# Value products in blocks of eight and four units, nine probability buffers, and another order at the end and in the norm, in an adaLN block with windowed attention

## The chip, the cores and the metric

The kernel runs on one core of one Trainium2 chip. The metric is device time in microseconds (us), measured from outside the program. The times shown are medians of a few runs. A profiled execution also gives its span, from the first to the last instruction on the core, which is a little shorter than the time of the same execution measured from outside.

## What is computed

The input is one sequence of S = 2048 rows with D = 448 features. The reference, cut to what matters:

```python
mod = (silu(c) @ w_mod).reshape(1, 6, 1, D)       # sa, ca, ga, sb, cb, gb
h = layernorm(x) * (1 + ca) + sa
qkv = h @ wqkv                                     # 16 heads of 28
scores = q @ k.T * 28 ** -0.5                      # key j is seen by query i if 0 <= i - j < 256
x = x + ga * (softmax(scores) @ v @ wo)
h = layernorm(x) * (1 + cb) + sb
x = x + gb * (mish(h @ w1 + b1) @ w2)              # w1: 448 x 1792
```

## The kernel before, in words

Each matrix product of width D is done in three passes: both operands are split into a high and a low part, and high x high, high x low and low x high are summed (`passes`, L205). The sequence is cut into four groups of 512 rows (`NG`, `GT`). The program is one list of instructions, written out by hand: a Python function issues an instruction when it is called, and each engine takes its own in the order in which they were issued (L76, a manual schedule). So the order of the calls is the schedule.

**Attention.** A group has 16 heads, and a group with a head is an item `i` (`NS` = 64 items). For each item the program does the following. `L` (L671) loads the item's queries and keys from a scratch tensor in DRAM. `A` (L680) makes the scores of 128 queries against 384 keys on the tensor engine (PE) into one of three banks `sA`, and the vector engine (DVE) takes the row maximum with the mask added (L689); there are four such quarters per item. After two items, `M1` (L697) splits the eight columns of maxima on DVE (L700, L701). `M2` (L703) transposes them on PE (tile `mt`, L705), copies the result on DVE (`mr`, L707), and sends it by DMA into two more rows of the query tile, so that a product of keys and queries comes out with the maximum already subtracted. `B` (L720) makes these transposed scores. An item has three units, and unit `u` covers one block set `b` of 512 columns (L22). `B` first puts the mask into the bank `sB`, either by PE with an identity matrix (L759) or, where `seeds(u)` is true, by a copy that the scalar engine (ACT) made two units earlier (L739). Then it multiplies (L731), and ACT takes the exponential into a tile `P` (L734).

Twelve units, three block sets of four heads, make a round `q`. There are 16 rounds, four to a group, and `r` is the unit's place in its round. `PV` (L761) multiplies the probabilities with the values: four heads fill the four column quarters of the array, each with 32 columns, into one bank `pv`. In the kernel before it is called once for each block set, that is for four units, at the places `PV_AT` (L1123): units 7, 9 and 13 counted from the start of the round. After the third, `EV` (L773) copies the sum out on ACT, `E` (L777) transposes it (tile `et`), and `E2` (L783) divides by the row sums on DVE.

**What stands between the units.** The loop at L1124 goes through the units. At each it calls `place` at up to six slots: the table `scores` (L1109) tells at which unit of the round and at which slot the 16 quarters `A` of the next round go, `M2_AT` (L1110) the same for `M2`, and `OUT_AT` (L1112) for `E` and `E2`. Between them a filler is drawn (`fill_main`, L994): the next group's projections to queries, keys and values (tiles `qk`, `qk_v`), and the last group's output projection (`ot`, `wo`). `RATE` (L1049) is how much filler a unit gets, one number for each group. `load_slot` (L1070) issues the loads of queries and keys on the DMA queue of SP, in which the DMA of `M2` stands too.

**Feed-forward.** The loop at L1227 goes through `NN` = 56 steps, 14 column blocks of 128 in each of the four groups. A step does `f1_mm` (11 products into a bank `z`, L970), `f1_act` (ACT: Mish into `t`, L976, and its high part `ah`, L977; DVE: the low part `al`, L978), and `ff2` of the step before (three products for each of four row tiles into four banks `acc`, L1191 to L1193). In the last step of a group, `ff2` also multiplies each bank with the gate (`yo`, L1197), adds the residual (L1200) and stores it. In the last group, three of these adds are on GpSimd (POOL), and the fourth is shared by DVE and POOL. The tiles `yo` come from three buffers with the tag `xr` (L548). A second filler (L1220) runs along in `fill_step` (L1222): what is left of the attention's output, and the second layer norm of the next group, whose transposes are 64 instructions on DVE, issued by fours (`blocks`, L892, the transposes at L897). In the first group a step draws it four times.

## Time and profile before

| | |
|---|---|
| time, median of 3 runs | 663.73 us (661.86, 663.73, 669.27) |
| the profiled execution | 668.01 us, span 666.2 us |
| PE, matmuls | 634.8 us busy, 3712 |
| DVE | 391.1 us busy, 1138 |
| ACT | 335.6 us busy, 584 |
| POOL | 120.6 us busy, 173 |
| mean granted clock of PE | 0.983 of full speed |

Rows of the timeline give the start, the duration, the engine, the line, the operation with the tiles it writes and reads, and how many instructions were merged into the row; in brackets stands how long the engine was idle before, and what ended that. Products of fp32 tiles appear as two hardware instructions each, so a block of eight `pv` products has 16 of them. A window's row gives the busy time of PE, of its weight loads (PEld), DVE, ACT and POOL, the granted clock of PE, and the DMA share and rate. Attention lasts from about 38 us to 366 us, and the feed-forward from there to the end.

### The profile page before, as it was taken

The page shows a single profiled execution, that of the slowest core. Times are in us where ns is not written, and L with a number is a line of the kernel's source. Part 1 is how long each engine was busy: PE and PEld are TensorE (multiplying, and loading weights), DVE is VectorE, ACT ScalarE, POOL GpSimd, SP SyncE. Part 2 cuts the span into 40 slices and gives each one's busy share as a digit, 9 for nine tenths or more (in the row PEclk, how much of TensorE's full clock was granted, in tenths as well). Part 3 has the DMA queues.
Part 4 walks back from the last instruction along what each step waited for, and adds up shares of the span by engine and source line. Part 5 has one row for each costly group of instructions (what it writes and reads, how often), then busy time and mean ns, then how long its engine had stood idle before and what let it go on. Part 6 is the DMA issues. An engine that isn't in the chain of part 4 may idle for free.

```text
span 666.2 us, 10727 instructions
## 1 busy us (share of the span) xinstructions
PE 634.8 (95%) x3712; PEld 514.3 (77%) x3712; DVE 391.1 (59%) x1138; ACT 335.6 (50%) x584; POOL 120.6 (18%) x173
## 2 busy tenths in 40 slices
PE   3998999999999999999988999999999999999996
PEld 3786777677887678877756898878888888888885
DVE  5765686675678767578777334954584438631112
ACT  4544567588875778635668633432233224323221
POOL 6652000043011200000030445340021001100002
PEclk9997999599999999999999999999999999999999
DMA  8786676547754478435852853003000300010001
GB/s 215 211 233 215 225 245 213 147 114 227 270 172 142 141 224 307 147 110 151 235 150 69 261 148 106 11 1 111 0 1 0 112 1 0 1 55 1 1 0 55
DMA packets 49169, 83.77 MB, mean 126 GB/s; under 512 B 5838, under 2 KB 27612, under 8 KB 49116
## 3 DMA queue, kind: packets, MB, share of 16 engines
q1 hardware_dynamic: 49116, 83.10, 40.6%
q8 instruction: 29, 0.48, 0.3%
q14 instruction: 24, 0.20, 0.1%
HBM read 53.45 MB, written 29.36 MB: 124 GB/s over the span
## 4 chain that ended last, share of the span: by engine, by line
PE 74%; issue 11%; DVE 8%; DMA 3%; ACT 2%; SPq 1%; POOL 1%; POOLq 0%; DVEq 0%; ACTq 0%
PE z L970 15%; PE qk L321 10%; PE pv L769 7%; PE sA L687 6%; PE sB L731 6%; PE wo L321 5%; PE acc L1193 4%; PE acc L1191 4%; PE acc L1192 4%; PE qk_v L321 4%; DVE yt L897 3%; DMA k<-scr 2%; PE sB L759 2%; DVE junk L689 1%; PE qk L506 1%
## 5 line engine op out<-in xcount | busy, mean ns | idle before, releaser
L689 DVE CUSTOM_DVE_ANT_0 junk<-sA,strip 128x384 bf16<-128x384 f32 (+2 forms) x256 | 135.4, 529 | 80.6 <-PE sA L687 65.8
L734 ACT ACTIVATE P<-sB 128x512 f32<-128x512 f32 (+2 forms) x192 | 108.3, 570 | 84.5 <-PE sB L731 82.1
L978 DVE TENSOR_TENSOR al<-t,ah 128x512 fp32r<-128x512 f32 x56 | 41.2, 735 | 137.2 <-ACT ah L977 136.9
L976 ACT ACTIVATE t<-z,b1c 128x512 f32<-128x512 f32 x56 | 38.4, 686 | 156.8 <-PE z L970 145.0
L970 PE MATMUL z<-hhf,w 128*128 128x512 f32 x224 | 88.9, 397 | 0.0
L970 PE MATMUL z<-hlf,w 128*128 128x512 f32 x224 | 88.8, 397 | 0.0
L731 PE MATMUL sB<-q,k 86*128 86x384 f32 (+1 forms) x352 | 87.2, 323 | 0.7 <-ACT sB L739 0.7
L687 PE MATMUL sA<-k,q 84*128 84x384 f32 (+2 forms) x256 | 82.4, 360 | 4.3 <-DMA k<-scr 2.7
L1193 PE MATMUL acc<-w2h,al 128*128 128x448 f32 x224 | 82.1, 366 | 1.9 <-DVE al L978 1.9
L1191 PE MATMUL acc<-w2h,ah 128*128 128x448 f32 x224 | 81.9, 366 | 0.0
L1192 PE MATMUL acc<-w2l,ah 128*128 128x448 f32 x224 | 81.8, 365 | 0.0
L731 PEld LDWEIGHTS sB<-q,k 86*128 86x128 f32 x352 | 60.3, 197 | 11.1 <-ACT sB L739 4.4
L970 PE MATMUL z<-hhf,w1l 128*128 128x512 f32 x168 | 66.5, 396 | 0.0
L897 DVE STREAM_TRANSPOSE yt<-xn 32x128 f32<-32x128 f32 x192 | 58.1, 302 | 2.6
L687 PEld LDWEIGHTS sA<-k,q 84*128 84x128 f32 x256 | 48.4, 197 | 10.4 <-DVE mx L689 2.7
L739 ACT ACTIVATE sB<-strip 128x512 f32<-128x512 bf16 (+2 forms) x95 | 54.6, 575 | 3.0
L769 PE MATMUL pv<-P,v 128*32 128x256 f32 (+2 forms) x704 | 50.2, 399 | 0.4 <-DVE on L790 0.4
L970 PEld LDWEIGHTS z<-hlf,w 128*128 128x128 f32 x224 | 42.1, 188 | 10.1
L970 PEld LDWEIGHTS z<-hhf,w 128*128 128x128 f32 x224 | 42.1, 188 | 9.1 <-issue 0.6
L1193 PEld LDWEIGHTS acc<-w2h,al 128*128 128x128 f32 x224 | 42.1, 188 | 5.9 <-DVE al L978 2.6
L1191 PEld LDWEIGHTS acc<-w2h,ah 128*128 128x128 f32 x224 | 42.1, 188 | 5.0
L1192 PEld LDWEIGHTS acc<-w2l,ah 128*128 128x128 f32 x224 | 42.1, 188 | 4.7
(155 smaller groups left out, 1029.1 us busy)
## 6 DMA issues: line engine op xcount, KB each, us to landing
k<-scr SPq DMA_DIRECT2D x48, 252.0 KB
q<-scr SPq DMA_DIRECT2D x64, 168.0 KB
scr<-st SPq DMA_DIRECT2D x21, 512.0 KB
scr<-st SPq DMA_DIRECT2D x29, 256.0 KB
x<-x1d SPq DMA_DIRECT2D x10, 448.0 KB
xin<-in_A_x_dram SPq DMA_DIRECT2D x8, 448.0 KB
xr<-in_A_x_dram SPq DMA_DIRECT2D x16, 224.0 KB
x1d<-xr SPq DMA_DIRECT2D x16, 224.0 KB
```

Of the source, the lines that this page charges most:

```text
L321: PE.matmul(p, b, a, start=(n == 0), stop=(n == 10))
L687: PE.matmul(p[:, c0:384], q[0:84, t * 128:(t + 1) * 128], k[0:84, t * 128 + c0:t * 128 + 384], start=True, stop=True)
L689: DVE.tensor_tensor_reduce(out=junk[:, c0:384], in0=p[:, c0:384], in1=mask[:, c0:384], scale=1.0, scalar=-3.0e38, op0=ALU.add, op1=ALU.max ...
L731: PE.matmul(p[:, c:c + 128 * (t1 - t0)], k[:, jj * 128:(jj + 1) * 128], q[:, t0 * 128:t1 * 128], start=False, stop=True, skip_group_check= ...
L734: ACT.activation(P[:, c0:], p[:, c0:], AF.Exp, scale=SCALE)
L739: ACT.activation(p[:, c0:], strip[:, c + c0:c + 512], AF.Copy)
L769: PE.matmul(pvb[q][32 * a:32 * a + 32, t0 * 128:t1 * 128], V[j % NV][:, h + a, :], Pt[4 * w + a][:, c:c + 128 * (t1 - t0)], start=(b == 0 ...
L897: DVE.transpose(y4[32 * j:32 * j + 32, ci, :, 32 * i:32 * i + 32], x4[32 * i:32 * i + 32, :, ci, 32 * j:32 * j + 32])
L970: PE.matmul(zb[n], ps[m][1], ps[m][0], start=(m == 0), stop=(m == 10))
L1191: PE.matmul(p, ah[n][:, ts], w2h[f], start=(f == 0), stop=False)
L1192: PE.matmul(p, ah[n][:, ts], w2l[f], start=False, stop=False)
L1193: PE.matmul(p, al[n][:, ts], w2h[f], start=False, stop=(f == NF - 1))
```

## The change

The places of `PV`. It is now called twice in a round, at units 9 and 13: first for the block sets 0 and 1 together (eight units of four heads), then for block set 2 (four units). The tile `P` gets nine buffers for seven. The 16 quarters `A` of a round, `M2` and `E` have other places, and the loop has other numbers of the mask copies that ACT makes (99 in all for 95). `RATE` has a number for each round instead of each group.

Here is PE's order in the first round, in which a block set has one piece for each head, with the block sets 0 and then 1. `pv` is the value product, `sA` are the quarters, `mt` the transposed maxima. Before, block set 0:

```order
L321 MATMUL qk_3_766<-hh_566,wq_88 128x512
L769 MATMUL pv_774<-P_661,v_152 32x384
L769 MATMUL pv_774<-P_677,v_152 32x384
L769 MATMUL pv_774<-P_698,v_152 32x384
L769 MATMUL pv_774<-P_714,v_152 32x384
L705 MATMUL mt_779<-ident,ms_740 16x128
```

and, some rows later, block set 1:

```order
L321 MATMUL qk_3_766<-hh_566,wq_88 128x512
L687 MATMUL sA_0_811<-k_7_381,q_3_393 128x128
L769 MATMUL pv_774<-P_728,v_154 32x256
L769 MATMUL pv_774<-P_746,v_154 32x256
L769 MATMUL pv_774<-P_755,v_154 32x256
L769 MATMUL pv_774<-P_787,v_154 32x256
L759 LDWEIGHTS identr
```

In the changed kernel:

```order
L321 MATMUL qk_3_763<-hh_566,wq_88 128x512
L687 MATMUL sA_0_806<-k_7_381,q_3_393 128x128
L687 MATMUL sA_1_809<-k_7_381,q_3_393 128x256
L770 MATMUL pv_812<-P_661,v_152 32x384
L770 MATMUL pv_812<-P_680,v_152 32x384
L770 MATMUL pv_812<-P_701,v_152 32x384
L770 MATMUL pv_812<-P_714,v_152 32x384
L770 MATMUL pv_812<-P_728,v_154 32x256
L770 MATMUL pv_812<-P_746,v_154 32x256
L770 MATMUL pv_812<-P_755,v_154 32x256
L770 MATMUL pv_812<-P_777,v_154 32x256
L687 MATMUL sA_2_821<-k_7_381,q_3_393 128x384
```

The first four products have moved down to the second four, with no other product between them, and `sA_1`, of the quarters, has moved up ahead of them, while `sA_2` follows directly behind. `mt` no longer stands behind a block of `pv`.

The feed-forward's filler. In the first group a step now draws it four times up to step 4, then five times, and three times as soon as the normalised tiles of the second group exist. This is DVE's order in that part: `L897`, in the changed kernel `L898`, are the transposes of the second group's norm, with their number at the end of the row, and `al` is the low part for the next `ff2`. Before:

```order
L897 STREAM_TRANSPOSE yt_5117<-xn_1_5046 32x4x32 x16
L978 TENSOR_TENSOR al_5212<-t_5213,ah_5211 128x512
L883 TENSOR_SCALAR yt_5117<-yt_5117,cols 128x512
L897 STREAM_TRANSPOSE yt_5117<-xn_1_5046 32x4x32 x16
L978 TENSOR_TENSOR al_5265<-t_5266,ah_5264 128x512
L883 TENSOR_SCALAR yt_5117<-yt_5117,cols 128x512
L897 STREAM_TRANSPOSE yt_5117<-xn_1_5046 32x4x32 x16
L978 TENSOR_TENSOR al_5318<-t_5319,ah_5317 128x512
L883 TENSOR_SCALAR yt_5117<-yt_5117,cols 128x512
L978 TENSOR_TENSOR al_5355<-t_5356,ah_5354 128x512
L978 TENSOR_TENSOR al_5389<-t_5390,ah_5388 128x512
L978 TENSOR_TENSOR al_5423<-t_5424,ah_5422 128x512
```

In the changed kernel:

```order
L898 STREAM_TRANSPOSE yt_5114<-xn_1_5043 32x4x32 x4
L982 TENSOR_TENSOR al_5249<-t_5250,ah_5248 128x512
L898 STREAM_TRANSPOSE yt_5114<-xn_1_5043 32x4x32 x12
L982 TENSOR_TENSOR al_5296<-t_5297,ah_5295 128x512
L884 TENSOR_SCALAR yt_5114<-yt_5114,cols 128x512
L898 STREAM_TRANSPOSE yt_5114<-xn_1_5043 32x4x32 x12
L982 TENSOR_TENSOR al_5345<-t_5346,ah_5344 128x512
L898 STREAM_TRANSPOSE yt_5114<-xn_1_5043 32x4x32 x4
L884 TENSOR_SCALAR yt_5114<-yt_5114,cols 128x512
L982 TENSOR_TENSOR al_5386<-t_5387,ah_5385 128x512
L982 TENSOR_TENSOR al_5420<-t_5421,ah_5419 128x512
```

Between two `al` stood 16 transposes and stand at most 12 now, and the last transposes come one `al` later.

The end. `ff2` of the steps 53, 54 and 55 is put off until the products `z` of step 55 are issued, and is then done row tile by row tile: two tiles of step 53 first, then for each row tile what is left of the three steps. `ah` and `al` of step 55 get buffers of another tag. The adds of the last group are all on DVE. PE's last 12 rows before were these (`acc3_0` to `acc3_3` are the banks of the four row tiles; `ah55` and `al55` are the parts of the last step):

```order
L1191 MATMUL acc3_0_6542<-w2h13_5394,ah55_6900 128x448
L1192 MATMUL acc3_0_6542<-w2l13_5395,ah55_6900 128x448
L1193 MATMUL acc3_0_6542<-w2h13_5394,al55_6901 128x448
L1191 MATMUL acc3_1_6543<-w2h13_5394,ah55_6900 128x448
L1192 MATMUL acc3_1_6543<-w2l13_5395,ah55_6900 128x448
L1193 MATMUL acc3_1_6543<-w2h13_5394,al55_6901 128x448
L1191 MATMUL acc3_2_6544<-w2h13_5394,ah55_6900 128x448
L1192 MATMUL acc3_2_6544<-w2l13_5395,ah55_6900 128x448
L1193 MATMUL acc3_2_6544<-w2h13_5394,al55_6901 128x448
L1191 MATMUL acc3_3_6545<-w2h13_5394,ah55_6900 128x448
L1192 MATMUL acc3_3_6545<-w2l13_5395,ah55_6900 128x448
L1193 MATMUL acc3_3_6545<-w2h13_5394,al55_6901 128x448
```

In the changed kernel 30 rows from the end:

```order
L1195 MATMUL acc3_0_6539<-w2h12_5350,ah54_6867 128x448
L1196 MATMUL acc3_0_6539<-w2l12_5351,ah54_6867 128x448
L1197 MATMUL acc3_0_6539<-w2h12_5350,al54_6868 128x448
L1195 MATMUL acc3_0_6539<-w2h13_5391,ah55_6885 128x448
L1196 MATMUL acc3_0_6539<-w2l13_5392,ah55_6885 128x448
L1197 MATMUL acc3_0_6539<-w2h13_5391,al55_6886 128x448
L1195 MATMUL acc3_1_6540<-w2h12_5350,ah54_6867 128x448
L1196 MATMUL acc3_1_6540<-w2l12_5351,ah54_6867 128x448
L1197 MATMUL acc3_1_6540<-w2h12_5350,al54_6868 128x448
L1195 MATMUL acc3_1_6540<-w2h13_5391,ah55_6885 128x448
L1196 MATMUL acc3_1_6540<-w2l13_5392,ah55_6885 128x448
L1197 MATMUL acc3_1_6540<-w2h13_5391,al55_6886 128x448
```

Row tile 0 is complete behind the sixth of these rows and row tile 1 behind the last; 18 rows for the tiles 2 and 3 follow, nine for each.

The whole diff:

```diff
@@ -546,7 +546,7 @@
     wol = [mid.tile([128, D], F32R, name=f"wol_{i}", tag="wo", bufs=7) for i in range(3)]
 
     def xr_tile(name):
-        return mid.tile([128, 512], F32, name=name, tag="xr", bufs=3)
+        return mid.tile([128, D], F32, name=name, tag="xr", bufs=3)
 
 
     def stg(pl, name):
@@ -730,7 +730,7 @@
         for jj, t0, t1, c in by_width(bl)[::-1]:
             PE.matmul(p[:, c:c + 128 * (t1 - t0)], k[:, jj * 128:(jj + 1) * 128], q[:, t0 * 128:t1 * 128],
                       start=False, stop=True, skip_group_check=True)
-        P = Pt[u] = att.tile([128, 512], F32, name=f"P{u}", tag="P", bufs=7)
+        P = Pt[u] = att.tile([128, 512], F32, name=f"P{u}", tag="P", bufs=9)
         ACT.activation(P[:, c0:], p[:, c0:], AF.Exp, scale=SCALE)
         if seeds(u + 2):
             p = sb[u + 2] = bank(f"sB{u % 2}", 1, f"sB{u + 2}")
@@ -741,7 +741,7 @@
     sb, known = {}, {}
 
     def seeds(u):
-        if not 12 <= u < NU or not ((0, 2730, 4095, 1365, 640, 4095, 4095, 1365, 0, 4095, 4095, 1365, 0, 1365, 84, 0)[u // 12] >> (u % 12)) & 1:
+        if not 12 <= u < NU or not ((0, 2746, 4095, 1365, 642, 4093, 4095, 1365, 0, 4095, 4095, 1367, 0, 1373, 592, 2048)[u // 12] >> (u % 12)) & 1:
             return False
         i, b = unit(u)
         return units(i // H, b)[0][3] >= known[u % 2]
@@ -759,16 +759,17 @@
             PE.matmul(p[:, c:c + n], identr, strip[:, m:m + n], start=(i == 0), stop=False, skip_group_check=True)
 
     def PV(w):
-        q, b = divmod(w, 3)
+        q, e = divmod(w, 2)
         g, h = divmod(4 * q, H)
-        if b == 0:
+        if e == 0:
             pvb[q] = bank("pv", 1, f"pv{q}")
-        for n, (jj, t0, t1, c) in enumerate(by_width(units(g, b))):
-            j = 4 * g - 2 + jj
-            for a in range(4):
-                PE.matmul(pvb[q][32 * a:32 * a + 32, t0 * 128:t1 * 128], V[j % NV][:, h + a, :],
-                          Pt[4 * w + a][:, c:c + 128 * (t1 - t0)],
-                          start=(b == 0 and n == 0), stop=False, skip_group_check=True)
+        for b in ((0, 1), (2,))[e]:
+            for n, (jj, t0, t1, c) in enumerate(by_width(units(g, b))):
+                j = 4 * g - 2 + jj
+                for a in range(4):
+                    PE.matmul(pvb[q][32 * a:32 * a + 32, t0 * 128:t1 * 128], V[j % NV][:, h + a, :],
+                              Pt[12 * q + 4 * b + a][:, c:c + 128 * (t1 - t0)],
+                              start=(b == 0 and n == 0), stop=False, skip_group_check=True)
 
     def EV(q):
         O4[q] = att.tile([128, GT], F32, name=f"o4_{q}", tag="o4")
@@ -971,7 +972,10 @@
 
     def f1_act(n):
         f = n % NF
-        ah[n], al[n] = ftile("ah", n, F32R), ftile("al", n, F32R)
+        if n == NN - 1:
+            ah[n], al[n] = (FW["ff"].tile([128, GT], F32R, name=f"{x}{n}", tag="stg", bufs=6) for x in ("ah", "al"))
+        else:
+            ah[n], al[n] = ftile("ah", n, F32R), ftile("al", n, F32R)
         t = ftile("t", n)
         ACT.activation(t, zb[n], AF.Mish, bias=FW["b1c"][:, f:f + 1])
         ACT.activation(ah[n], t, AF.Copy)
@@ -1046,14 +1050,14 @@
         if not (told.get(i) == "bank" and pipe.held() or told.get(i) == "dve" and two):
             told[i] = next(side[i], None)
 
-    RATE = (0.76, 1.01, 0.88, 0.45)
+    RATE = (0.76, 0.76, 0.72, 0.76, 1.01, 1.01, 1.01, 1.09, 0.92, 0.96, 0.91, 0.88, 0.45, 0.6, 0.45, 0.41)
     FRONT = (0, 1, 3, 0)
     ln1 = {g: gen_ln1(g, g == 1) for g in range(1, NG)}
     fillers = {g: fill_main(g) for g in range(NG)}
     side = (fill_early(), fill_late())
 
-    def step(g):
-        return next(fillers[g], 99.0) or RATE[g]
+    def step(g, q):
+        return next(fillers[g], 99.0) or RATE[q]
 
     def need(keys, g):
         if all((g, m) in done for m in keys):
@@ -1106,10 +1110,10 @@
             load_slot(4 + i)
     later[:0] = late
     credit = 0.0
-    scores = {(0, 3): [0], (0, 4): [1], (2, 0): [2], (2, 5): [3], (3, 0): [4], (4, 0): [5], (4, 5): [6], (5, 0): [7], (6, 1): [8], (6, 3): [9], (7, 3): [10], (8, 3): [11], (8, 5): [12], (9, 1): [13], (9, 5): [14], (10, 1): [15]}
-    M2_AT = {(7, 0): 0, (11, 3): 1}
-
-    OUT_AT = {(3, 5): E, (4, 2): E2}
+    scores = {(0, 3): [0], (0, 5): [1], (1, 0): [2], (1, 4): [3], (3, 0): [4], (4, 0): [5], (4, 4): [6], (5, 0): [7], (6, 1): [8], (7, 0): [9], (7, 5): [10], (8, 3): [11], (8, 5): [12, 13], (9, 0): [14], (9, 1): [15]}
+    M2_AT = {(7, 1): 0, (11, 4): 1}
+
+    OUT_AT = {(4, 1): E, (4, 2): E2}
 
     def place(q, r, slot):
         if (r, slot) in OUT_AT and 0 < q <= NS // 4:
@@ -1120,7 +1124,7 @@
             A(4 * q + 4 + n // 4, n % 4)
         if (r, slot) in M2_AT:
             M2(2 * q + 2 + M2_AT[r, slot])
-    PV_AT = {4 * w + (7, 5, 5)[w % 3]: w for w in range(NU // 4)}
+    PV_AT = {12 * q + (9, 13)[e]: 2 * q + e for q in range(NS // 4) for e in range(2)}
     for u in range(NU + 7):
         s, k = divmod(u, 3)
         g = s // H
@@ -1131,8 +1135,8 @@
         w = PV_AT.get(u)
         if w is not None:
             PV(w)
-            if w % 3 == 2:
-                EV(w // 3)
+            if w % 2:
+                EV(w // 2)
         q, r = divmod(u, 12)
         place(q, r, 0)
         if u < NU:
@@ -1149,10 +1153,10 @@
                 chunk["v"] = 4 if v == 0 and g or 0 < g < NG - 1 else 2
             if v == 0:
                 credit = 0.0
-            credit += RATE[g] * (2 if v < FRONT[g] else 1)
+            credit += RATE[q] * (2 if v < FRONT[g] else 1)
             n = 0
             while credit > 0.0:
-                credit -= step(g)
+                credit -= step(g, q)
                 n += 1
                 if n == 1:
                     place(q, r, 3)
@@ -1181,11 +1185,11 @@
     FW["ff"] = ff
     p1, gbn = FW["p1"], FW["gbn"]
 
-    def ff2(n):
+    def ff2(n, tiles=range(4)):
         g, f = divmod(n, NF)
         if f == 0:
             acc[g] = [bank("acc", 4, f"acc{g}_{t}") for t in range(4)]
-        for t in range(4):
+        for t in tiles:
             ts = slice(t * 128, (t + 1) * 128)
             p = acc[g][t][:, 0:D]
             PE.matmul(p, ah[n][:, ts], w2h[f], start=(f == 0), stop=False)
@@ -1195,9 +1199,7 @@
                 j = 4 * g + t
                 y = xr_tile(f"yo{j}")[:, 0:D]
                 DVE.tensor_tensor(y, p, gbn, op=ALU.mult)
-                for eng, a, b in (((DVE, 0, D),) if g < NG - 1 else ((POOL, 0, D),) if t < 3 else
-                                  ((DVE, 0, 256), (POOL, 256, D))):
-                    eng.tensor_tensor(y[:, a:b], y[:, a:b], x1[g][:, t, a:b], op=ALU.add)
+                DVE.tensor_tensor(y, y, x1[g][:, t, :D], op=ALU.add)
                 dma(of[j * 128:(j + 1) * 128, :], y)
 
     def gen_x1_ln2(g):
@@ -1241,8 +1243,14 @@
             pieces(n)
         if n:
             fill_step()
-            ff2(n - 1)
-            for _ in range(2 + (g == 0)):
+            if n == NN:
+                ff2(n - 3, (0, 1))
+                for t in range(4):
+                    for last in range(n - 3 + (t < 2), n):
+                        ff2(last, (t,))
+            elif n < NN - 2:
+                ff2(n - 1)
+            for _ in range(2 + (g == 0 and 1 not in XN2) * (1 + (n > 4))):
                 fill_step()
     for st in (ff_s, mid_s, cst_s, FW["s"], psf_s):
         st.close()
```

## The prediction, made before the changed kernel ran

> **What bounds the kernel now.** I read the head of the page first, then the chain that ended last.
>
> ```profile
> PE 634.8 (95%) x3712; PEld 514.3 (77%) x3712; DVE 391.1 (59%) x1138; ACT 335.6 (50%) x584; POOL 120.6 (18%) x173
> PE 74%; issue 11%; DVE 8%; DMA 3%; ACT 2%; SPq 1%; POOL 1%; POOLq 0%; DVEq 0%; ACTq 0%
> ```
>
> PE is busy 95% of the span and makes up 74% of the chain, so what counts is time on PE: work taken off it, and waits of it that end sooner. Next I asked for windows, to see whether that holds in every stage.
>
> ```profile
> 118.00:136.00 18.00, 17.46 (x102) 12.39 (x95) 11.53 (x42) 10.59 (x18) 2.54 (x2) 0.62 0.44 128
> 300.00:367.00 67.00, 61.11 (x524) 43.78 (x524) 51.22 (x156) 45.63 (x83) 7.76 (x13) 1.00 0.53 150
> 600.00:640.00 40.00, 40.00 (x186) 34.53 (x185) 5.54 (x8) 10.50 (x17) 0.00 (x0) 1.00 0.00 1
> ```
>
> The feed-forward (third row) is PE throughout. The last attention group (second row) is not: PE is idle 5.9 of 67 us there, with DVE busy 51. In the first row PE is busy, but at a granted clock of 0.62, for reasons to which I come back. PE's own waits name what it lacks:
>
> ```profile
> PE mt L705 <- DVE ms L701: 4.1, 3, 2.3
> PE sA L687 <- DMA k<-scr: 2.7, 3, 1.1
> PE acc L1193 <- DVE al L978: 1.9, 2, 1.1
> PE sA L687 <- DVE mx L689: 1.6, 2, 0.8
> ```
>
> The columns are the total, the number of times and the longest. All are small, so this change can win only small sums in several places. About 1% is what a measurement of this kernel can tell from no change.
>
> **Value products.** The change removes no product; it makes 32 blocks of 48. So the question is what a block costs apart from its products.
>
> ```profile
> 84.32 0.85 PE L769 MATMUL pv<-P,v 128*32 128x384 f32 x8
> 85.11 0.28 PE L705 MATMUL mt<-ident,ms 128*16 128x128 f32 x1
> 262.46 0.35 PE L687 MATMUL sA<-k,q 84*128 84x384 f32 x1
> 262.65 0.37 PE L321 MATMUL qk_v<-wq,hl 128*128 128x448 f32 x1
> 263.26 0.34 PE L687 MATMUL sA<-k,q 84*128 84x384 f32 x1
> 263.53 1.07 PE L769 MATMUL pv<-P,v 128*32 128x128 f32 x16
> 264.53 0.28 PE L705 MATMUL mt<-ident,ms 128*16 128x128 f32 x1
> ```
>
> From the start of a block to the start of what follows, a block with 384 columns for each head takes 85.11 - 84.32 = 0.79 us, and one with 512 (128 and 384) 264.53 - 263.53 = 1.00 us. So 128 columns cost 0.21 us, 384 cost 0.63, and 0.16 us is left that doesn't depend on the columns: it lies at the block's end. At its start, `pv` begins 0.27 us behind an `sA`, where an ordinary product begins 0.19 us behind the same `sA`: 0.08 us more. A block thus costs 0.24 us for itself, whatever it holds. Sixteen blocks fewer are 3.8 us. One is saved in each round. I count 14 of them, 3.4 us: of the four in the last group, where PE waits anyway, two may only lengthen a wait. The bounds are 0 (every saved piece turns into a wait) and 3.8 us. Nothing new is waited for: the first block now stands at unit 9 and needs the exponentials up to unit 7, which is what the second block at unit 9 needed before, and nine buffers `P` hold units 0 to 8.
>
> **Mask copies.** Four more masks in all are made by ACT.
>
> ```profile
> 340.16 0.34 PE L759 MATMUL sB<-strip,identr 128*128 128x128 bf16 x2
> 340.26 0.48 PE L731 MATMUL sB<-q,k 86*128 86x384 f32 x2
> L739 ACT ACTIVATE sB<-strip x95: 387/602/602, 74.2 to 342.6; 128x512 f32<-128x512 bf16 x79, 128x384 f32<-128x384 bf16 x8, 128x256 f32<-128x256 bf16 x8
> ```
>
> On PE a mask costs 0.10 us (start to start of the two rows), so 0.4 us goes. ACT gets 4 x 0.60 = 2.4 us; PE hides it, as ACT is busy half of the span. Without that cover it would be a loss of 2.0 us net.
>
> **The norm in the feed-forward's first group.** Here PE waits for `al`, and the timeline of DVE and PE shows why.
>
> ```profile
> 427.26 5.04 DVE L897 STREAM_TRANSPOSE yt<-xn 32x128 f32<-32x128 f32 x16
> 432.33 0.69 DVE L978 TENSOR_TENSOR al<-t,ah 128x512 fp32r<-128x512 f32 x1
> 431.94 0.36 PE L1192 MATMUL acc<-w2l,ah 128*128 128x448 f32 x1
> 433.08 0.47 PE L1193 MATMUL acc<-w2h,al 128*128 128x448 f32 x1 [0.77 <-DVE al L978]
> 438.00 0.36 PE L1192 MATMUL acc<-w2l,ah 128*128 128x448 f32 x1
> 439.47 0.47 PE L1193 MATMUL acc<-w2h,al 128*128 128x448 f32 x1 [1.10 <-DVE al L978]
> 493.32 3.79 DVE L897 STREAM_TRANSPOSE yt<-xn 32x128 f32<-32x128 f32 x12
> 497.14 0.69 DVE L978 TENSOR_TENSOR al<-t,ah 128x512 fp32r<-128x512 f32 x1
> 659.02 0.37 PE L1192 MATMUL acc<-w2l,ah 128*128 128x448 f32 x1
> 659.23 0.36 PE L1193 MATMUL acc<-w2h,al 128*128 128x448 f32 x1
> ```
>
> Sixteen transposes take 5.04 us and stand ahead of `al` in DVE's queue, so a step's DVE work exceeds PE's step and DVE falls behind. The two products of `al` start 1.14 and 1.47 us behind their neighbour, where 0.21 us is usual (last two rows): 0.93 + 1.26 = 2.2 us lost. With twelve at most, as the order now has it, the transposes take 3.79 us; that is how the second group runs already (rows at 493), and no wait for `al` is listed there. I take the whole 2.2 us. The bounds are 0 and 2.2, with a loss possible too: the last transposes come one `al` later, and if the split that follows them were late for the second group's first products, up to one such wait, 1.3 us, would come back. The drawing faster up front puts two output rows between two `al`, which lies in the slack that those steps have.
>
> **The end.**
>
> ```profile
> 654.55 0.37 PE L1191 MATMUL acc<-w2h,ah 128*128 128x448 f32 x1
> 656.13 0.69 DVE L978 TENSOR_TENSOR al<-t,ah 128x512 fp32r<-128x512 f32 x1 [4.32 <-ACT ah L977]
> 657.79 1.85 DVE L1197 TENSOR_TENSOR yo<-acc,gbn 128x448 f32<-128x448 f32 x3 [0.97 <-PE acc L1193]
> 661.73 0.62 DVE L1197 TENSOR_TENSOR yo<-acc,gbn 128x448 f32<-128x448 f32 x1 [2.08 <-DMA out_dram<-yo]
> 662.43 0.83 POOL L1200 TENSOR_TENSOR yo<-yo,x 128x192 f32<-128x192 f32 x1 [0.62 <-DVE yo L1197]
> 659.67 3.95 SPq L59 DMA_DIRECT2D out_dram<-yo  x4
> L1200 DVE TENSOR_TENSOR yo<-yo,x x13: 425/625/627, 452.0 to 662.4; 128x448 f32<-128x448 f32 x12, 128x256 f32<-128x256 f32 x1
> ```
>
> PE ends at 659.23 + 0.36 = 659.59. The fourth tile then stands idle until 661.73, because its buffer is the first tile's, whose store was issued only at 659.67, 2.06 us earlier. Its last add ends at 662.43 + 0.83 = 663.26. In the new order row tile 0 is complete 24 products before the end, 24 x 0.21 = 5.0 us, so its buffer is free about 659.59 - 5.0 + 0.62 + 0.63 + 2.06 = 657.9, 1.7 us before the fourth tile wants it. The last tile then takes 0.62 + 0.63 us behind PE and is ready at 660.84: 2.4 us sooner. Against it stands a new wait. `al` of step 55 ends at 656.82, 2.27 us behind the first product that follows `z`; its first reader is now the twelfth product, 11 x 0.21 = 2.3 us behind, and its weights must be loaded ahead of that, so about 0.2 us is waited. Net 2.2 us; bounds 0 (the buffer is late after all) and 2.4.
>
> **Places and rates.** Quarters, `M2`, `E` and filler move. The clearest effect is on two waits of the kind below.
>
> ```profile
> 116.34 0.34 PE L687 MATMUL sA<-k,q 84*128 84x384 f32 x1
> 117.47 0.44 PE L687 MATMUL sA<-k,q 84*128 84x384 f32 x1 [0.79 <-DVE mx L689]
> 344.67 0.44 PE L687 MATMUL sA<-k,q 84*128 84x384 f32 x1 [0.76 <-DVE mx L689]
> 351.89 0.28 PE L705 MATMUL mt<-ident,ms 128*16 128x128 f32 x1 [1.26 <-DVE ms L701]
> ```
>
> The last quarter of a round moves from unit 10 to unit 9 and `M2` from slot 3 to slot 4 of unit 11, so the maxima have a unit more: I take 1.3 us for the wait at 351.89. Behind a late `mt` stand its copy on DVE and, on SP's queue, the DMA of `mr` and the loads of the next queries and keys. Moving it by a slot delays them by the filler of a unit at most, some 0.8 us, which a DMA already in flight covers. `E` goes behind one quarter and one `B`, and DVE's division waits for it a little longer. For all of this I have no row, so the bounds are the last group's whole idle time, a gain of 5.9 us, and as much lost. I stay near the one row that answers directly. The smaller `xr` tile and the other tag of `ah` change memory only.
>
> **Sum:** 3.4 + 0.4 + 2.2 + 2.2 + 1.3 = 9.5 us off the profiled execution's 668.0, to 658.5. That execution lies 4.3 us above the median of the runs shown, 663.7, and the stretch at low clock may explain it. Hardly anything of my terms lies in that stretch, so I carry the difference over: 663.7 - 9.5 = 654.2 us.
>
> **The clock.** The first window above lost 18 x (1 - 0.62) = 6.8 us. It sets in just behind the wait at 116.34, where the filler has run out, `sA` follows `sA`, and the longest wait for anything is 0.79 us. The Trainium skill (TensorE: Matmul & The Clock Gate, Part 1) has the clock halved only after a whole idle window of some 3.4 us. By that rule no such dip could come from waits like these, and rival 3 below would have no chance; the trace disagrees, at 0.62.
>
> **Rivals.** (1) The attention gives nothing: what PE no longer spends at the blocks' ends it spends waiting for DVE, which is busy 51 of 67 us in the last group. For it speak the waits for `mx`; against it that PE's listed waits for DVE in attention sum to no more than 5.7 us (4.1 and 1.6). Then only the norm and the end remain: 663.7 - 4.4 = 659.3, within 1%. Chance 0.24. (2) The waits of the last group go, 5.9 us for my 1.3: 654.2 - 4.6 = 649.6. Against it, several of them are for DMA, which the change leaves alone. Chance 0.12. (3) Slower, by the clock. Between units 1 and 9 no value products stand any more, so in rounds with little filler (3, and 12 to 15) quarters follow each other with nothing that lets DVE catch up, and waits gather ahead of unit 9. Each further dip costs 6.8 us. One leaves 661.0; from the second on it decides: 654.2 + 13.6 = 667.8, and with three 674.6, slower by 1.6%. For it speaks the dip that is there; against it that the waits at 344 and 351 set off none. Chance 0.05 for two or more. The forecast itself, with its terms two thirds to all there, has 0.59 and a range of its own of 650.5 to 658.
>
> **How the numbers follow.** Faster by over 1% means below 657.1: most of the forecast (0.53 of its 0.59) and rival 2, 0.65. The rest of the forecast and rival 1 and part of rival 3 are within 1%: 0.32. Slower 0.03. For 8 in 10 the range takes in the middle of rival 2 and of rival 1, and one added dip: 648 to 661.
>
> **What would show it.** In the new profile, 32 blocks `pv` with 0.24 us each beside their products; no wait of `acc` for `al` near 430 to 440; the last `yo` product within 0.1 us of PE's end and the last store issued about 1.3 us behind it; `mt` no longer waiting about 1.3 us for `ms` in the last group. I am wrong if PE's idle time between 300 and 367 us grows by what the blocks save, if a clock well under 1.00 stands in a stage that had 1.00, or if the first products of a feed-forward group wait for the norm.

## The result and the profile after

The changed kernel takes 658.66 us (median of 19 executions, 655.40 to 663.63); the kernel before, run beside it, 667.32 (19 executions, 661.44 to 669.76). The ratio is 0.9896, with a 95% interval of 0.9873 to 0.9918: 6.9 us less (5.5 to 8.5). (The two medians are 8.7 us apart, a little more than that interval allows; the ratio is what I go by.) The sign and the range of the prediction hold. Its sum of 9.5 us is too large, and two of its five terms hang on each other, which a sum can't show. The experiments below show that.

The profiled execution has a span of 653.4 us, against 666.2 before, so its difference of 12.8 us is more than the change brings: 3.9 us of PE's cycles are lost to a low clock in it, span x (1 - 0.994), against 11.3 before, span x (1 - 0.983). First the head of its page, then its chain.

```profile
PE 628.5 (96%) x3705; PEld 514.5 (79%) x3705; DVE 393.8 (60%) x1141; ACT 337.5 (52%) x588; POOL 116.5 (18%) x169
PE 85%; DVE 6%; ACT 4%; issue 2%; POOL 1%; DMA 1%; DVEq 0%; POOLq 0%; ACTq 0%
```

PE has 85% of the chain instead of 74%. Of what PE still waits for, these are the rows that matter here (total, times, longest; left out are 9.4 us for the first input at the start and some waits of the output projection):

```profile
PE mt L705 <- DVE ms L701: 3.0, 3, 2.3
PE sB L759 <- ACT P L734: 1.8, 6, 0.5
PE sB L731 <- ACT sB L739: 1.7, 3, 1.1
PE sA L687 <- DVE mx L689: 0.6, 3, 0.2
PE sB L731 <- DMA q<-mr: 0.5, 1, 0.5
PE acc L1196 <- POOL w2l L941: 0.4, 1, 0.4
```

The waits for `k` by DMA (2.7) and for `al` (1.9) are gone, and those for `mx` fell from 1.6 to 0.6. That of `k` isn't the change's doing for certain: it is 1.4 and 1.6 us in two other kernels with the attention of before, and 0.9 and 1.8 us in two that differ from the changed kernel in a few masks only. ACT is waited for more: `sB` waits 3.5 us for exponentials and mask copies, where it waited 1.5, and the feed-forward has a wait of 0.4 us for POOL's `w2l`. In the same stretch that stood at a clock of 0.62, the clock is now 1.00 (first row; the second is explained behind it).

```profile
118.00:136.00 18.00, 16.91 (x142) 11.90 (x145) 14.39 (x49) 15.19 (x27) 6.27 (x6) 1.00 0.46 130
118.00:136.00 18.00, 17.53 (x110) 12.08 (x109) 12.01 (x41) 12.90 (x23) 4.19 (x4) 0.74 0.43 123
```

The second row is from the kernel with the attention's part of the change alone (run `e_attn` below): the same attention, and a clock of 0.74. So the change doesn't do away with that dip; this one execution was without it.

A block in the timeline of PE, block sets 0 and 1 together:

```profile
263.03 0.69 PE L687 MATMUL sA<-k,q 84*128 84x384 f32 x3
263.65 1.93 PE L770 MATMUL pv<-P,v 128*32 128x128 f32 x32
265.51 0.44 PE L687 MATMUL sA<-k,q 84*128 84x384 f32 x1
```

It holds two times 512 columns for each head and takes 265.51 - 263.65 = 1.86 us; eight times the prediction's 0.21 and its 0.16 at the end are 1.84. So the products and the block's end cost what was said, however much the block holds, and there are 32 of them. (The 0.08 us at the start don't show in these rows.) The end, on PE, DVE and SP's queue:

```profile
643.41 0.36 PE L1196 MATMUL acc<-w2l,ah 128*128 128x448 f32 x1
643.71 0.47 PE L1197 MATMUL acc<-w2h,al 128*128 128x448 f32 x1
648.69 0.36 PE L1197 MATMUL acc<-w2h,al 128*128 128x448 f32 x1
649.09 0.62 DVE L1201 TENSOR_TENSOR yo<-acc,gbn 128x448 f32<-128x448 f32 x1 [0.55 <-PE acc L1197]
649.75 0.63 DVE L1202 TENSOR_TENSOR yo<-yo,x 128x448 f32<-128x448 f32 x1
645.53 5.21 SPq L59 DMA_DIRECT2D out_dram<-yo  x4
```

PE ends at 648.69 + 0.36 = 649.05 and DVE starts on the fourth tile at 649.09: no wait for a buffer. The last add ends at 650.38, 1.33 us behind PE, and PE's end to the span's end is 653.36 - 649.05 = 4.3 us, where it was 6.65. The new wait for `al` of step 55 is 643.71 - 643.41 = 0.30 us between starts where 0.21 is usual: 0.1 us.

### The profile page after: what moved, and what is told of

Read it like the earlier page. It is cut to its first block, busy times and chain, and to the rows that moved or that the text cites. A ratio compares the mean times of both kernels' runs of the same rounds, so it can differ in the third digit from the quotient of the medians.

```text
span 653.4 us, 10706 instructions
## 1 busy us (share of the span) xinstructions
PE 628.5 (96%) x3705; PEld 514.5 (79%) x3705; DVE 393.8 (60%) x1141; ACT 337.5 (52%) x588; POOL 116.5 (18%) x169
## 4 chain that ended last, share of the span: by engine, by line
PE 85%; DVE 6%; ACT 4%; issue 2%; POOL 1%; DMA 1%; DVEq 0%; POOLq 0%; ACTq 0%
PE z L971 21%; PE qk L321 10%; PE acc L1197 7%; PE acc L1196 7%; PE acc L1195 7%; PE sA L687 6%; PE pv L770 6%; PE wo L321 5%; PE sB L731 5%; PE qk_v L321 5%; DVE junk L689 3%; ACT P L734 2%; PE sB L759 2%; PE qk L506 1%; PE et L781 1%
## 5 line engine op out<-in xcount | busy, mean ns | idle before, releaser
L687 PE MATMUL sA<-k,q 84*128 84x384 f32 (+2 forms) x256 | 84.3, 363 | 1.7 <-DVE mx L689 0.6
L731 PE MATMUL sB<-q,k 86*128 86x384 f32 (+1 forms) x352 | 83.5, 312 | 2.2 <-ACT sB L739 1.7
L687 PEld LDWEIGHTS sA<-k,q 84*128 84x128 f32 x256 | 47.6, 191 | 23.6 <-DVE mx L689 14.1
L898 DVE STREAM_TRANSPOSE yt<-xn 32x128 f32<-32x128 f32 x192 | 58.0, 302 | 2.7
L739 ACT ACTIVATE sB<-strip 128x512 f32<-128x512 bf16 (+2 forms) x99 | 56.8, 574 | 3.1
L770 PE MATMUL pv<-P,v 128*32 128x256 f32 (+2 forms) x704 | 45.5, 388 | 0.0
```

The source lines that it names most:

```text
L687: PE.matmul(p[:, c0:384], q[0:84, t * 128:(t + 1) * 128], k[0:84, t * 128 + c0:t * 128 + 384], start=True, stop=True)
L731: PE.matmul(p[:, c:c + 128 * (t1 - t0)], k[:, jj * 128:(jj + 1) * 128], q[:, t0 * 128:t1 * 128], start=False, stop=True, skip_group_check= ...
L739: ACT.activation(p[:, c0:], strip[:, c + c0:c + 512], AF.Copy)
L770: PE.matmul(pvb[q][32 * a:32 * a + 32, t0 * 128:t1 * 128], V[j % NV][:, h + a, :], Pt[12 * q + 4 * b + a][:, c:c + 128 * (t1 - t0)], start ...
L898: DVE.transpose(y4[32 * j:32 * j + 32, ci, :, 32 * i:32 * i + 32], x4[32 * i:32 * i + 32, :, ci, 32 * j:32 * j + 32])
```

## Experiments

Each ratio is against executions of the kernel before beside it on the same chip. Since effects are below 1%, I read the traces in two more ways. "Idle" is the length of the attention, from the first `sB` to the first `acc`, less PE's busy time in it, both from a window's row. The profile models the ends of products, so short waits may hide in the busy time. "Round" is the time from the last value product of a round to that of the next; it repeats within 0.1 us from kernel to kernel in many rounds where nothing is changed and the clock is full.

### The three parts by themselves

The end alone, in the kernel before:

```diff
+        if n == NN - 1:
+            ah[n], al[n] = (FW["ff"].tile([128, GT], F32R, name=f"{x}{n}", tag="stg", bufs=6) for x in ("ah", "al"))
...
+            if n == NN:
+                ff2(n - 3, (0, 1))
+                for t in range(4):
+                    for last in range(n - 3 + (t < 2), n):
+                        ff2(last, (t,))
+            elif n < NN - 2:
+                ff2(n - 1)
```

> The kernel before with the change's end alone: the last ah and al in other buffers, the last three steps' products by row tile, the last group's adds on DVE. My theory: the fourth row tile no longer waits for its buffer. The last yo product starts within 0.1 us of PE's end, PE's end to the span's end falls from 6.65 to about 4.4 us, 2.2 us off the whole, a ratio of 0.9967. Rival: the first row tile's store lands too late, or the wait for al of step 55 grows to about 2 us: then the time stays, 1.000.

Measured: 0.9956 (0.9922 to 0.9991).

```profile
653.18 0.36 PE L1196 MATMUL acc<-w2h,al 128*128 128x448 f32 x1
653.58 0.62 DVE L1200 TENSOR_TENSOR yo<-acc,gbn 128x448 f32<-128x448 f32 x1 [0.55 <-PE acc L1196]
654.24 0.62 DVE L1201 TENSOR_TENSOR yo<-yo,x 128x448 f32<-128x448 f32 x1
```

DVE starts 0.04 us behind PE's end (653.18 + 0.36), and the span ends at 657.84, 4.3 us behind PE: 2.3 us off. My theory.

The norm alone, in the kernel before:

```diff
-            for _ in range(2 + (g == 0)):
+            for _ in range(2 + (g == 0 and 1 not in XN2) * (1 + (n > 4))):
```

> The kernel before with the change's pacing of the norm alone. My theory: at most twelve transposes stand between two al, the two products that started 0.93 and 1.26 us late no longer do, 2.2 us off, a ratio of 0.9967. Rival A, from the trace of the changed kernel: a wait of acc for w2l of POOL comes in at the start of the group, about 0.5 us, and 1.7 us are left, 0.9975. Rival B: the waits only move to other steps of the group, 1.000. The rows of the two al products and of all of PE's gaps from 420 to 500 us tell them apart; the times alone hardly.

Measured: 0.9969 (0.9936 to 1.0003), so the time alone doesn't tell it from no change. On DVE and PE:

```profile
428.75 3.79 DVE L897 STREAM_TRANSPOSE yt<-xn 32x128 f32<-32x128 f32 x12
432.57 0.69 DVE L978 TENSOR_TENSOR al<-t,ah 128x512 fp32r<-128x512 f32 x1
429.77 0.47 PE L1192 MATMUL acc<-w2l,ah 128*128 128x448 f32 x1 [0.37 <-POOL w2l L940]
```

Twelve transposes at most between two `al`, as forecast, and no wait for `al`; the wait for POOL is the only one left from 420 to 460 us. From the first `acc` to PE's end, the trace has 286.5 us against 288.3 before: 1.7 us, rival A. The changed kernel has the same wait.

All attention edits, without the two others; the diff starts from the changed kernel, and the edits of the end are taken back with it:

```diff
-            for _ in range(2 + (g == 0 and 1 not in XN2) * (1 + (n > 4))):
+            for _ in range(2 + (g == 0)):
...
-                DVE.tensor_tensor(y, y, x1[g][:, t, :D], op=ALU.add)
+                for eng, a, b in (((DVE, 0, D),) if g < NG - 1 else ((POOL, 0, D),) if t < 3 else
+                                  ((DVE, 0, 256), (POOL, 256, D))):
+                    eng.tensor_tensor(y[:, a:b], y[:, a:b], x1[g][:, t, a:b], op=ALU.add)
```

> The kernel before with the attention's part of the change alone: blocks, nine P, masks, places, rates, the smaller xr. The prediction's terms for it are 3.4 + 0.4 + 1.3 = 5.1 us, a ratio of 0.9924. Rival 1, what the blocks save is waited: 1.000 by time, with PE's idle time between 300 and 367 us up by about 3. Between them, from the trace of the changed kernel: waits of sB for ACT take back 1.5 to 2 us, leaving 3 to 3.5 us, 0.995. The three parts should add up to the whole change, 0.9896: if this one comes out at 0.9924 the terms of the prediction hold, at 0.996 the whole has more than its parts.

Measured: 0.9950 (0.9928 to 0.9973), 3.3 us, the case between the two theories. The three parts give 0.0044 + 0.0031 + 0.0050 = 0.0125, and the whole 0.0104: they add up within their intervals. What fell short is the attention, 3.3 us for 5.1.

### The blocks

The changed kernel with three blocks a round:

```diff
-    PV_AT = {12 * q + (9, 13)[e]: 2 * q + e for q in range(NS // 4) for e in range(2)}
+    PV_AT = {4 * w + (7, 5, 5)[w % 3]: w for w in range(NU // 4)}
...
-        for b in ((0, 1), (2,))[e]:
-            for n, (jj, t0, t1, c) in enumerate(by_width(units(g, b))):
+        for n, (jj, t0, t1, c) in enumerate(by_width(units(g, b))):
```

> The changed kernel with the value products in three blocks a round again, at units 7, 9 and 13 of the next round, with all else of the change kept. My theory: 16 more blocks at 0.24 us are 3.8 us; from the changed kernel's 0.9896 it goes to 0.9953 of the kernel before. Rival: the shorter PE work only waits for ACT and DVE, so that giving the blocks back shortens those waits by the same amount: 0.990 to 0.991, and PE's busy time is up by about 3.8 us while PE's listed waits for ACT and DVE in attention fall by as much.

Measured: 0.9914 (0.9879 to 0.9949); the interval takes in both theories. The clock blurs it too: these eight executions lost 2.5 us to a low clock in the mean (span x (1 - clock)), those of the changed kernel 5.6. The rounds say more. Here are rounds 1 to 15 together, with three blocks a round and then in the changed kernel, from the last value product of round 0 to that of round 15, at full clock in both:

```profile
74.59:360.70 286.11, 278.17 (x2043) 212.67 (x2036) 206.88 (x681) 204.00 (x372) 31.93 (x43) 1.00 0.61 186
74.33:357.31 282.98, 275.32 (x2043) 214.63 (x2036) 206.42 (x681) 203.43 (x372) 31.89 (x43) 1.00 0.61 188
```

Fifteen blocks more make it 3.1 us longer, 0.21 us a block, and PE's busy time has 2.85 of that. So the price holds, and the rival, by which the saved time is only waited, doesn't. Round by round it is less even: 5, 6, 7, 9, 10 and 11 are 0.29 to 0.35 us longer; 1, 4, 12 and 14, where PE waits, 0.1 to 0.4 us shorter; and round 13 is 1.9 us longer, 1.3 of it waits of `sA` for the DMA of `k`, which the changed kernel doesn't have there.

This run is also the other places, rates and masks with the blocks of before. The end and the norm alone make 1 - 0.0044 - 0.0031 = 0.9925, so with three blocks a round these bring 0.0011, or 0.7 us, with an interval of some 4 us to both sides.

The kernel before with the two blocks alone, and nine `P` and the smaller `xr` that they need:

```diff
+    PV_AT = {12 * q + (9, 13)[e]: 2 * q + e for q in range(NS // 4) for e in range(2)}
+        for b in ((0, 1), (2,))[e]:
...
+        P = Pt[u] = att.tile([128, 512], F32, name=f"P{u}", tag="P", bufs=9)
```

> The kernel before with the blocks of value products alone: two a round, at units 9 and 13, nine buffers P, the smaller xr; places, rates and masks as before. My theory: each saved block is 0.24 us on PE, 14 to 16 of them are 3.4 to 3.8 us, a ratio of 0.9946, and the attention from its first sB to the first acc gets shorter by as much as in the run of all attention edits (3.8 us where both are taken at full clock). Rival: without new places PE waits for what it saved, since the last quarter at unit 10 and M2 stand as before: 1 us or less, 0.9985, and PE's waits for mx and ms in the last group grow by 2 to 3 us.

Measured: 1.0088 (1.0060 to 1.0115), 5.9 us slower. Neither theory had that. Idle time, here and in the changed kernel:

```profile
53.73:372.43 318.70, 304.21 (x2202) 234.03 (x2200) 219.04 (x729) 215.20 (x393) 33.53 (x44) 0.98 0.60 184
```

```profile
52.45:362.37 309.92, 302.05 (x2194) 234.75 (x2193) 219.68 (x729) 217.48 (x397) 33.18 (x44) 0.99 0.61 190
```

The first row is the blocks alone, the second the changed kernel: 14.5 us idle (318.70 - 304.21) against 7.9. With the attention of before it is 9.6 to 10.7 (10.4 in the kernel with the end alone). One of the places, on DVE and PE:

```profile
134.30 0.56 DVE L689 CUSTOM_DVE_ANT_0 junk<-sA,strip 128x384 bf16<-128x384 f32 x1
134.90 0.50 DVE L700 CAST ms<-mx 128x8 fp32r<-128x8 f32 x1
135.44 0.17 DVE L701 TENSOR_TENSOR ms<-mx,ms 128x8 fp32r<-128x8 f32 x1
134.26 0.42 PE L687 MATMUL sA<-k,q 84*128 84x384 f32 x1
135.66 0.28 PE L705 MATMUL mt<-ident,ms 128*16 128x128 f32 x1 [0.97 <-DVE ms L701]
```

From the start of `sA` to the start of `mt` it takes 1.40 us, nearly all of it DVE's work. In the kernel before, the 1.00 us of the block at unit 7 stood between the two (row at 264.53 of the prediction: `mt` behind `pv`). The block was cover, that is, work of PE behind which another engine's work is hidden; taking it away uncovered the maxima. In the whole trace `mt` now waits 7 times where it waited 3 times (7.3 us in all for 5.2 in the kernel with the end alone).

That doesn't account for all of it. Idle time grew by 4.1 us and the blocks should save 3.4 to 3.8. The clock adds about 1.4: these executions lost 9.9 us to it and those of the kernel before beside them 7.1, and a lost microsecond costs about 0.5 us of time (worked out under "The clock" below). That makes about 2 us of the 5.9. Where the rest lies is open, so the lost cover is shown at places like this one, and as the whole cause it is argued.

### Places, rates and masks

The changed kernel with the old places and rates:

```diff
-    RATE = (0.76, 0.76, 0.72, 0.76, 1.01, 1.01, 1.01, 1.09, 0.92, 0.96, 0.91, 0.88, 0.45, 0.6, 0.45, 0.41)
+    RATE = (0.76,) * 4 + (1.01,) * 4 + (0.88,) * 4 + (0.45,) * 4
...
-    M2_AT = {(7, 1): 0, (11, 4): 1}
+    M2_AT = {(7, 0): 0, (11, 3): 1}
-    OUT_AT = {(4, 1): E, (4, 2): E2}
+    OUT_AT = {(3, 5): E, (4, 2): E2}
```

(and the 16 places of quarters of before).

> The changed kernel with the places of quarters, M2 and E and the four rates of before. My theory was that places and rates are worth 1.3 us: 0.9896 goes to 0.9915 of the kernel before, and mt waits about 1.3 us for ms in the last group again. Rival, from the runs of the first batch (all attention edits 3.8 us, blocks 3.5): they are worth 0.3 us or less, 0.990; the wait for ms comes back but others (sB for ACT) go.

Measured: 1.0061 (1.0036 to 1.0086). Places and rates are worth 0.0165 of the time, 11 us, and not 1.3 or 0.3, once the blocks are there; with three blocks a round they brought about 0.7. Idle time is 15.3 us.

The old table of masks in the changed kernel (the tuple in `seeds`), and then two masks of round 14 taken from ACT:

```diff
-(0, 2746, 4095, 1365, 642, 4093, 4095, 1365, 0, 4095, 4095, 1367, 0, 1373, 592, 2048)
+(0, 2730, 4095, 1365, 640, 4095, 4095, 1365, 0, 4095, 4095, 1365, 0, 1365, 84, 0)
```

> The changed kernel with the table of masks of before. My theory: four masks go back to PE, 0.4 us more, 0.9902. Rival: ACT's mask copies hold PE up (sB waits for ACT's copy 1.7 us in the changed kernel, 1.53 of it at units 4 and 6 of round 14, which both tables give to ACT): then the time is the same or up to 0.5 us less, 0.989, with other waits for ACT.

Measured: 0.9900 (0.9871 to 0.9930), as the changed kernel.

```diff
-        (... 0, 1373, 592, 2048)
+        (... 0, 1373, 512, 2048)
```

> The changed kernel with the masks of units 4 and 6 of round 14 made by PE and not by ACT. In the changed kernel PE waits 0.45 and 1.08 us there for ACT's copies. If the copies are what holds PE up (0.60 us each behind the exponential of two units earlier), both waits shrink to nearly nothing, for 0.2 us of products: 1.3 us less than the changed kernel, 0.9876. Rival: the exponential itself is late there, ACT being behind: each wait shrinks by the copy's 0.60 at most, 0.45 + 0.60 - 0.2 = 0.85 us, 0.9883; or what is saved is waited for at the next mt or sA, nothing, 0.9896.

Measured: 0.9908 (0.9881 to 0.9936): nothing gained. In the trace the waits of `sB` for ACT's copies did fall, from 1.7 to 0.2 us, but that brings no time that can be seen. Masks decide nothing that can be measured here, and no kernel of this study is faster than the changed one.

### Which of places and rates

The blocks alone, with M2 moved as in the change:

```diff
-    M2_AT = {(7, 0): 0, (11, 3): 1}
+    M2_AT = {(7, 1): 0, (11, 4): 1}
```

> The kernel before with the blocks alone, as in the run of the blocks alone (1.0088), and M2 at slot 1 of unit 7 and slot 4 of unit 11. My theory now: the block at unit 7 hid the 1.40 us from the last sA to mt (maximum 0.56, sum of maxima, two small copies); without it mt waits 0.97 us at 135.66 and less elsewhere, some 3 us in all of the 4 us by which PE's idle time between the first sB and the first acc grew (10.5 to 14.5 us). With M2 behind the scores of unit 7 these waits go: idle time falls to about 11.5 us and the ratio to 1.004. Rival: the maxima are late whatever M2's slot, since the quarter before it is placed at slot 3 of unit 6: the wait only moves into the next sA or sB, idle time stays at 14, 1.0088.

Measured: 1.0096 (1.0058 to 1.0134), idle 15.7 us. My theory that M2's slot is the cure falls: at 135.41 `mt` still starts 0.93 us behind the `sB` that now stands ahead of it, 0.65 us of it idle.

The other way round, the changed kernel with M2's old slots (the same two lines reversed):

> The changed kernel with M2 at slot 0 of unit 7 and slot 3 of unit 11, as before. Same theory: mt stands behind sA again and waits about 0.9 us in the rounds with little filler, 2 to 3 us in all: 0.9896 goes to 0.9935. Rival: M2's slots don't matter and the places of quarters do: 0.990.

Measured: 0.9905 (0.9870 to 0.9939), idle 9.4 us. Again the rival.

The changed kernel with the old places of quarters and E:

```diff
-    scores = {(0, 3): [0], (0, 5): [1], (1, 0): [2], (1, 4): [3], ... (7, 0): [9], (7, 5): [10], (8, 3): [11], (8, 5): [12, 13], (9, 0): [14], (9, 1): [15]}
+    scores = {(0, 3): [0], (0, 4): [1], (2, 0): [2], (2, 5): [3], ... (6, 3): [9], (7, 3): [10], (8, 3): [11], (8, 5): [12], (9, 1): [13], (9, 5): [14], (10, 1): [15]}
```

> The changed kernel with the places of quarters and of E as before. Of the 10.9 us by which the old places and rates together made it longer (1.0061 against 0.9896) M2 should have about 3. If quarters at unit 10, behind the block at unit 9, are what keeps the maxima and the next mt late, most of the rest is here: 6 us, 0.999. Rival: the rates have it, since the filler of the last group is spent early at 0.45 a unit and later rounds have none: then 0.991 here and 0.999 with the old rates.

Measured: 1.0006 (0.9984 to 1.0028), idle 14.1 us. In the attention PE waits:

```profile
PE mt L705 <- DVE ms L701: 6.2, 7, 2.3
PE sB L731 <- ACT sB L739: 2.2, 2, 1.3
PE sA L687 <- DVE mx L689: 1.6, 4, 0.7
```

The changed kernel has 3.0 in its whole span for the first of these. So the places of quarters (and E) are needed, and with them DVE gets its time back; the last quarter now stands at slot 1 of unit 9 in place of slot 1 of unit 10.

The changed kernel with four rates (its `RATE` line as in the diff above):

> The changed kernel with the four rates of before. If the rates have most of the rest: 0.999. If the places of quarters have it: 0.991. Half each: 0.995 in both runs. In every case PE's idle time by group tells where: the rates alone can move idle time between the rounds of one group.

Measured: 1.0077 (1.0047 to 1.0107), no better than the old places and the old rates together (1.0061). Its waits for `ms` are few; it has another one:

```profile
259.36 0.40 PE L731 MATMUL sB<-q,k 86*128 86x256 f32 x2
263.35 0.66 PE L687 MATMUL sA<-k,q 84*128 84x384 f32 x1 [3.59 <-DMA k<-scr]
253.70 1.72 SPq L59 DMA_DIRECT2D scr<-st  x2
255.52 1.24 SPq L59 DMA_DIRECT2D q<-scr  x1
256.81 0.79 SPq L59 DMA_DIRECT2D k<-scr  x1
258.07 0.39 SPq L59 DMA_DIRECT2D k<-scr  x1
```

```profile
256.00:260.00 4.00, 3.76 (x23) 3.36 (x22) 3.75 (x12) 3.79 (x8) 0.00 (x0) 1.00 0.95 288
260.00:264.00 4.00, 0.65 (x2) 0.68 (x3) 0.93 (x3) 1.09 (x2) 0.00 (x0) 0.88 0.93 303
264.00:268.00 4.00, 4.00 (x14) 3.63 (x13) 2.07 (x7) 1.74 (x3) 0.00 (x0) 0.50 0.69 262
```

At 0.88 a unit the filler of rounds 8 and 9 runs later. The keys are stored and loaded just ahead of the quarter that needs them, with the DMA engines busy 0.95. Each item has one load of `k` and four quarters, in the same order, so the load that this quarter waits for is the one issued at 256.81 (that at 258.07 is the next item's). PE is ready for `sA` at 259.76, 2.95 us behind the issue. In the changed kernel the same item's load is issued at 250.43 and its first quarter starts at 258.79, 8.4 us behind. PE stands idle for 3.59 us, and then the clock is at half for 6.83 us. That `k` is late is shown. Why it is issued late is argued: behind the DMA of `mr` at 250.36 three loads of `wm` and four stores stand ahead of it in SP's queue, and in the changed kernel one load of `wm` only. The kernel with the old places and the old rates has no such stall (its round 10 takes 22.1 us), so it comes from the new places with the old rates. The rounds of five kernels (us; * with half clock in it):

```
round   end alone  blocks alone  all attention edits  old quarters  old rates
  5       22.04       21.82            21.93              21.88        21.93
  6       21.65       21.40            21.40              21.43        21.40
 10       21.98       22.13            21.03              21.09        28.45*
 11       25.24       24.97            22.74              23.63        25.13
 12       17.23       18.09            17.51              18.12        17.51
 14       15.44       17.86*           14.78              16.42*       15.85
 15       13.20       14.00            13.02              14.54        14.23
```

Rounds 5 and 6, full of filler, show the blocks as they were reckoned: 0.22 and 0.25 us less (9 and 11 do so too). Rounds with little filler or with waits of their own show the lost cover: blocks alone are 0.8 us longer or more in 12 and in 15. Round 11 shows the rates: 2.5 us less, part of which rounds 8 and 9 give back.

## Why the prediction was right, and where it was not

**The end** (2.2): right, 2.3 in the trace of the changed kernel and in that of the end alone, with 0.1 of the 0.2 us allowed for `al`.

**The norm** (2.2): mechanism right, size 1.6 to 1.7 by the traces, since a wait of 0.4 us for POOL's `w2l`, which I had not looked for, comes in.

**Value products** (3.4): the price of 0.24 us a block is right. The step that failed is "Nothing new is waited for". I asked whether the later block's inputs were there, and not what the block at unit 7 had hidden. My own rows showed it: `mt` behind `pv`, 1.00 us. By itself this part is 5.9 us slower, below the bound of 0 that I set. Rival 3 had it in words, that without value products between units 1 and 9 the quarters follow each other "with nothing that lets DVE catch up" and waits gather, but I put it down as a matter of the clock, at a chance of 0.05 for two dips or more, and didn't carry it into this term. With the places moved along, as the change does, the step does no harm: there the blocks bring 3.1 us in rounds 1 to 15.

**Places and rates** (1.3, bounds -5.9 to 5.9): this term has no one size. The wait of `mt` in the last group is gone, as said. With the blocks of before they bring about 0.7 us, not told from nothing. Given the new blocks they bring 11 us, and the quarters' places and the rates are both needed: with either one undone the change is worth nothing or less (1.0006, 1.0077). I priced them one by one against the trace of before, where the cover was still there. Later, behind the run of the blocks alone, I took M2's slot for the part that mattered; two runs show that it doesn't.

So the split depends on the order in which the parts are put in. Blocks first, they are -5.9, and places and rates then bring 9.2 (1.0088 to 0.9950); places first, they bring about 0.7 and the blocks then 3.1 by the rounds (by the ratios 1.2, with some 3 us to both sides), near my 1.3 and 3.4. That the two terms could be added at all was luck: I gave no reason for it, and the middle step of the first order is slower than the start. The attention as a whole brings 3.3 us for my 5.1 (masks included, whose 0.4 can't be seen). The rest, waits for ACT and in group 1 about 1 us of idle time where there was 0.1, is rival 1 in part.

**The sum** is 9.5 for 6.9 (5.5 to 8.5). The time of 654.2 is 4.5 us below the median of 658.66, and 3.6 of that is the base: 663.73 was the median of three executions, and 667.32 is that of 19.

**The clock** (rival 3): not in this change, but the mechanism was real. In its 19 executions the mean loss, span x (1 - clock), is 5.6 us; in 30 of the kernel before that ran beside the first kernels, 7.1; in the six with the blocks alone, 9.9. The price was too high: a straight line through 67 executions of the kernel before rises by 0.5 us for each lost microsecond, and in rounds 3 and 14 it costs 0.5 to 0.9 of time (round 3 is 17.98 us with 5.46 lost in the profile of before, and 15.10 with none in that of the norm alone; that waits shrink as PE slows would explain it, but wasn't tried).

## What to carry to other kernels

Before you move work off the bound engine, look at what stands behind it: a block that costs time may also be what another engine's result is waited out in, and the gain may only be there when the waiting work is moved along with it. Before you add up the terms of one schedule, ask whether each would stand without the others; to see it, undo each in the new kernel and do each alone in the old. Where an order is tuned as a whole, a sum in the right range doesn't show that its terms are right.

## What the runs showed of the hardware

The granted clock goes by windows of 3.41 us. In the 14 traces of this case every stretch at half clock, other than the last one, which the program's end cuts off, is 3.41 us long or a multiple (6.83, 10.24, 13.65). I laid windows of that length on the same grid and compared PE's busy share in a window with the clock of the next, from 40 us on, without the end. Of 2442 windows at full clock 29 were followed by half. The busy share was 0.55 or less in 10 windows, 9 of them followed by half; 0.75 or less in 83, 28 of them; above 0.80 in 2322, none of them. In the profile of the norm alone:

```profile
334.23:337.65 3.42, 3.42 (x25) 3.07 (x23) 2.22 (x7) 2.93 (x7) 0.57 (x1) 1.00 0.75 195
337.65:341.06 3.41, 1.99 (x21) 1.27 (x23) 3.13 (x12) 2.63 (x5) 3.15 (x5) 1.00 0.81 241
341.06:344.47 3.41, 3.41 (x22) 1.93 (x15) 2.19 (x9) 0.61 (x2) 0.25 (x1) 0.50 0.03 6
```

The longest wait listed in the middle window is 0.76 us: several short ones in one window are enough (busy 1.99 of 3.41), and the next window is at half. So the Trainium skill's rule (TensorE: Matmul & The Clock Gate, Part 1), a whole idle window, has the length of window that the traces show, but asks for more idle time than was needed here. Only the stall with four rates, 3.59 us, comes near to that rule. Where the grid falls against the program's start differs from trace to trace, which may be one reason why the time of one and the same kernel varies by some microseconds; that wasn't tried. Which measure of activity the gate uses these traces don't settle.
